# A planned order for attention and SwiGLU: PSUM banks given out one by one, and offsets for five stages

## The chip, the cores and the metric

The kernel runs on one core of a Trainium2 chip. Time is device time in microseconds (us), from the start of an execution to its end. The engines are TensorE (PE: matmuls and transposes; its weight loads, PEld, have rows of their own), VectorE (DVE), ScalarE (ACT), GpSimd (POOL) and SyncE (SP, which here only issues DMAs). Each engine works through its own list of instructions in order and waits on semaphores. TensorE writes to PSUM, which has eight banks of 512 fp32 columns by 128 partitions here; VectorE and ScalarE empty them.

## What is computed

Eight batches of eight heads, 576 positions, head size 64, in fp32:

```python
scores = scale * np.matmul(q, k.transpose(0, 1, 3, 2))
thresh = np.max(scores, axis=-1, keepdims=True) - tau
scores = np.where(scores >= thresh, scores, -1000000000.0)
attn = np.exp(scores - max); attn = attn / (sum(attn) + 1e-09)
x = (attn @ v), heads joined: 4608 rows of 512
xn = x / sqrt(mean(x * x) + 1e-06) * rms_g
g = xn @ w_gate; val = xn @ w_val            # 512 -> 1536
out = (g * sigmoid(g) * val) @ w_out         # 1536 -> 512
```

(The last lines of the softmax and the joining of heads are shortened here.)

## The kernel before

**Work units.** The 4608 rows are cut into 36 chunks of 128 rows: for each batch four chunks of main rows, and for each pair of batches one chunk ("v") made of the last 64 rows of both. A chunk has four steps, one per pair of heads, so there are 144 steps. A step is:

- Scores (L697, `emit_burst`): fp32 matmuls of 64x64 tiles into `s_ps[0]` and `s_ps[1]`, one tile per head, 576 columns each. For steps 0 to 31 a burst is one step; from step 32 on scores are cut into bursts of 1024 columns without regard to steps (`CHOP`, `plan_bursts` L743). A burst fills two banks of each head, and its matmuls follow one another on PE.
- Row maxima (L730, `ttr`): VectorE reads the scores from PSUM, writes them negated and scaled to `ssb`, and takes the extreme in the same instruction (`mx`, or `mxp` where a step's row is cut by a burst).
- Threshold (L771, `nthr`, POOL), masking (L782, `prelu`, ACT), exponential to fp16 (L789, `ex2`, ACT).
- Transposes of the weights `wsb` to `wt`: for the first 16 steps on TensorE (L834, copied out by VectorE, L843), then by DMA (L849).
- For each two steps: attention times v (L870 and L875, `emit_av`), with the row sums in an extra column, and division by them on VectorE (L892, L893).

After a chunk's four steps `emit_x` (L900) squares and sums (ACT, L910), takes the power (POOL), scales (POOL) and transposes x to `xnT` by DMA. The chunks form ten groups (`SIZES`: 2, 2 and eight times 4). `emit_ffn` takes a group at a time: 12 slices of the hidden size, each with a gate product (L976, `gmm`) and a value product (L981, `vmm`), tanh on ACT (L990), two VectorE instructions (L993 `silu`, L998 `gate`) to `hf`, and then per chunk 12 output products in two runs of six (L1047, `omm`), a copy (L1062 or L1064, `ev`) and a store. In the last group output products are streamed slice by slice (L1022). Weights come in by 12 loads of 512 KB and are cast on POOL (L1133); `wo` comes by POOL's own DMAs (L1145).

The start has a path of its own (`emit_first`, L422): loads of batch 0, transposes on TensorE (L462), copies by ACT and DVE (L472). `setup` (L287) zeroes a tile for eight warm-up matmuls (L291, L292, L299) and fills constant columns of `va` (L309 to L311, `vconst`).

**PSUM.** Score banks are two tiles of 1024 columns, so four banks. The other four are the "ring", which serves transposes, attention outputs and FFN products. After the last step's maxima the score banks are opened to the ring as well (`OPENS`); `SLOTS` and `ACC` say which banks ordinary users and the streamed last group may have. Semaphores between engines follow the data in the banks; the planner below decides order and bank numbers only.

**The planner.** Nothing is emitted directly. Each piece of work is an `Op` with an engine, an estimated cost, a due time `prio` (in steps), and dependences. `order_ops` (L56) simulates the engines: at each point, the operation that can start first goes next, and where several of an engine can start at the same moment, the one with the lowest `prio`. To `prio` the table `RANK` adds an offset per engine and kind of work, one number for all of the run, for due times of 8 and later; SP's operations get none. FFN slices have due times of their own: group by group, never before the step after which the group is complete plus `LAG` 8, 12 slices over 16 steps for a full group. A change between fp32 score matmuls and other kinds is charged `SWITCH`. Bursts depend on all maxima of the burst before (`last_ttr`), a maximum on the whole burst (`made`). A user of the ring gets the bank that has been free longest. In the end the operations' functions are called in the planned order, which fixes every engine's list.

Of the kernel before, what the change touches and what calls it, by code (L numbers as in the profile page):

```python
# [23 lines left out]
SWITCH = 125.0  # L24

RANK = dict(
    ACT={"emit_ffn/ev": 450, "emit_ffn/store": 110, "emit_ffn/tanh": -300, "emit_k_tail/ev": -210, "emit_q_tail/ev": -80, "emit_qk/ev": 370,
        "emit_softmax/ex2": 60, "emit_softmax/prelu": 220, "emit_x/sq": -330},
    DVE={"emit_blocks/turn_k": 120, "emit_blocks/turn_kt": 288, "emit_blocks/turn_q": 293, "emit_burst/ttr": -57.4, "emit_ffn/ev": 320,
        "emit_ffn/gate": 60, "emit_ffn/silu": -59, "emit_k_tail/ev": 80, "emit_qk/ev": -20, "emit_softmax/ev": 320, "emit_x/ev": 50},  # L30
    PE={"emit_av/fn": -370, "emit_burst/fn": 16, "emit_ffn/gmm": 20, "emit_ffn/omm": 23, "emit_ffn/vmm": -40, "emit_k_tail/tr": 210, "emit_q_tail/tr":
        -160, "emit_qk/tr": 60, "emit_softmax/tr": -40, "emit_x/trp": 20},
    POOL={"emit_block_loads/swap": 40, "emit_softmax/nthr": -240, "emit_x/mean": -150, "emit_x/norm": -10, "round_/<lambda>": 130, "main/<lambda>":
        700, "main/cast": -280},
# [3 lines left out]
class Op:  # L38
    __slots__ = ("eng", "cost", "prio", "deps", "fn", "ring", "frees", "slot", "end", "start", "dma", "opens", "nring", "mode", "bulk", "release", "pick", "quad", "lat")

    def __init__(self, eng, cost, prio, deps, fn, ring=None, frees=None, dma=0.0, nring=1, mode=0, bulk=False):
        self.eng, self.cost, self.prio, self.fn = eng, cost, prio, fn
        self.deps = [d for d in deps if d is not None]
        self.ring, self.frees, self.dma = ring, frees, dma
        self.slot = self.end = self.start = None
        self.opens = ()
        self.nring = nring
# [8 lines left out]
def order_ops(ops, ring_sizes):  # L56
# [4 lines left out]
    for o in ops:  # L61
        if o.prio >= 8.0 and o.eng != "SP":
            path = o.fn.__qualname__.split(".")
            o.prio += RANK.get(o.eng, {}).get((path[-3] if path[-3].startswith(("emit", "load", "setup", "transposed", "round")) else "main") + "/" + path[-1], 0.0)

    ring_free = {r: [(0.0, i) for i in range(n)] for r, n in ring_sizes.items()}
    users = {}
    left = {}
    for i, o in enumerate(ops):
        left[i] = len(o.deps)  # L70
        for d in o.deps:
            users.setdefault(id(d), []).append(i)
# [10 lines left out]
    while len(out) < len(ops):  # L83
# [35 lines left out]
        if o.ring is not None:  # L119
# [5 lines left out]
            if o.pick:  # L125
                o.slot.sort()
# [1160 lines left out]
```

## Time and profile before

Three runs took 533.15, 534.36 and 535.47 us; the median is 534.36. The profiled execution's own span, from its first instruction to its last, is 532.2 us; the median lies 2.2 us above it, which takes in what lies around the instructions and the difference between executions.

| | before |
|---|---|
| span of the profiled execution | 532.2 us |
| median of three runs | 534.36 us |
| PE busy | 521.9 us (98%) |
| DVE busy | 465.9 us (88%) |
| ACT busy | 443.6 us (83%) |
| POOL busy | 224.9 us (42%) |
| mean granted TensorE clock | 0.997 |
| instructions | 14401 |
| longest chain, share by engine | PE 68%, DVE 11%, ACT 10%, no visible wait 4%, DMA 3% |

A profile row gives a line of the kernel, engine, operation, what it writes and reads, a count, busy time and the mean of one; then idle time before it on its engine and what ended that. Matmuls are pipelined and the end of one is modelled, so rows of consecutive matmuls overlap and PE looks busier than it is. The time from one start to the next is more reliable, and the chain of waits gives it: there each piece is cut where the next begins. "PEld <- DVE" is a weight load that waited for VectorE. "issue" is time for which the profile shows no wait.

### The profile page before, as it was taken

The page shows a single profiled execution, that of the slowest core. Times are in us where ns is not written, and L with a number is a line of the kernel's source. Part 1 is how long each engine was busy: PE and PEld are TensorE (multiplying, and loading weights), DVE is VectorE, ACT ScalarE, POOL GpSimd, SP SyncE. Part 2 cuts the span into 40 slices and gives each one's busy share as a digit, 9 for nine tenths or more (in the row PEclk, how much of TensorE's full clock was granted, in tenths as well). Part 3 has the DMA queues.
Part 4 walks back from the last instruction along what each step waited for, and adds up shares of the span by engine and source line. Part 5 has one row for each costly group of instructions (what it writes and reads, how often), then busy time and mean ns, then how long its engine had stood idle before and what let it go on. Part 6 is the DMA issues. An engine that isn't in the chain of part 4 may idle for free.

```text
span 532.2 us, 14401 instructions
## 1 busy us (share of the span) xinstructions
PE 521.9 (98%) x5368; PEld 275.4 (52%) x5368; DVE 465.9 (88%) x1348; ACT 443.6 (83%) x648; POOL 224.9 (42%) x478
## 2 busy tenths in 40 slices
PE   8999999999999999999999999999999999999996
PEld 4666666654555454545454544454545454454442
DVE  4899989979999799989997999999999898865741
ACT  5999999989997899889987898989999999962210
POOL 2368777424762165727733265726662111111000
PEclk9999999999999999999999999999999999999998
DMA  9999999979977788999889898999897678653013
GB/s 196 237 282 289 239 159 180 182 150 230 181 162 165 166 170 182 157 223 182 170 167 180 146 175 174 203 210 166 174 195 137 119 118 134 128 112 70 13 29 99
DMA packets 218886, 88.51 MB, mean 166 GB/s; under 512 B 195264, under 2 KB 204992, under 8 KB 218816
## 3 DMA queue, kind: packets, MB, share of 16 engines
q1 hardware_dynamic: 216016, 85.49, 81.1%
q0 software_dynamic: 1600, 1.57, 1.9%
q8 instruction: 42, 0.69, 0.5%
q10 hardware_dynamic: 1200, 0.52, 0.5%
q14 instruction: 28, 0.23, 0.1%
HBM read 37.75 MB, written 9.44 MB: 89 GB/s over the span
## 4 chain that ended last, share of the span: by engine, by line
PE 68%; DVE 11%; ACT 10%; issue 4%; DMA 3%; POOL 1%; SPq 1%; DVEq 0%; ACTq 0%; POOLq 0%
PE s_ps L697 21%; PE ring L1047 13%; PE ring L981 11%; PE ring L976 11%; DVE ssb L730 6%; ACT ssb L782 5%; PE ring L875 4%; ACT wsb L789 3%; PE s_ps L1022 2%; ACT th L990 2%; DVE sl L993 2%; PE ring L870 1%; DMA stg<-in_moe_w_gate_dram 1%; DMA wt<-wsb 1%; PE s_ps L981 1%
## 5 line engine op out<-in xcount | busy, mean ns | idle before, releaser
L782 ACT ACTIVATE ssb<-ssb,nth 128x576 f32<-128x576 f32 x288 | 209.3, 766 | 21.5 <-POOL nth L771 21.0
L730 DVE CUSTOM_DVE_ANT_0 ssb<-s_ps,zcol 128x576 f32<-128x576 f32 (+8 forms) x288 | 169.5, 636 | 6.3 <-PE s_ps L697 5.5
L697 PE MATMUL s_ps<-qkt 64*64 64x288 f32 (+8 forms) x2256 | 170.8, 412 | 1.1 <-DVE mx L730 0.8
L789 ACT ACTIVATE wsb<-ssb 128x1152 f16<-128x1152 f32 x144 | 166.7, 1158 | 2.5 <-DMA wt<-wsb 0.3
L697 PEld LDWEIGHTS s_ps<-qkt 64*64 64x64 f32 x2256 | 81.9, 134 | 66.4 <-issue 28.2
L976 PE MATMUL ring<-xnT,wg 128*128 128x512 f16 (+1 forms) x464 | 109.2, 358 | 0.6 <-DVE sl L993 0.5
L981 PE MATMUL ring<-xnT,wv 128*128 128x512 f16 (+1 forms) x456 | 106.9, 357 | 0.5 <-DVE sl L993 0.2
L990 ACT ACTIVATE th<-ring 128x512 f32<-128x512 f32 (+1 forms) x116 | 62.5, 541 | 39.4 <-PE ring L976 39.0
L771 POOL TENSOR_SCALAR nth<-mx 128x2 f32<-128x2 f32 x144 | 31.0, 215 | 151.0 <-DVE mx L730 141.0
L993 DVE SCALAR_TENSOR_TENSOR sl<-th,ring 128x512 f32<-128x512 f32 (+1 forms) x116 | 72.1, 623 | 11.3 <-ACT th L990 11.2
L981 PEld LDWEIGHTS <-wv 128*128 128x128 f16 x480 | 44.6, 98 | 50.2 <-issue 11.1
L976 PEld LDWEIGHTS <-wg 128*128 128x128 f16 x480 | 43.0, 98 | 52.6 <-issue 15.1
L730 DVE CUSTOM_DVE_ANT_0 ssb<-s_ps,zcol,mxp 128x128 f32<-128x128 f32 (+7 forms) x112 | 52.9, 510 | 13.2 <-PE s_ps L697 13.0
L875 PE MATMUL ring<-va,wt 128*128 128x65 f16 (+1 forms) x1280 | 51.1, 193 | 0.0
L875 PEld LDWEIGHTS <-wt 128*128 128x128 f16 (+1 forms) x1280 | 46.1, 100 | 5.0 <-issue 0.6
L1047 PE MATMUL ring<-wo,hf 128*128 128x512 f16 x204 | 47.7, 379 | 0.0
L998 DVE TENSOR_TENSOR stg<-ring,sl 128x512 f16<-128x512 f32 (+1 forms) x57 | 35.6, 628 | 2.4
L998 DVE TENSOR_TENSOR hf<-ring,sl 128x512 f16<-128x512 f32 (+1 forms) x57 | 35.5, 627 | 1.8
L1047 PE MATMUL ring<-wo,stg 128*128 128x512 f16 x156 | 36.5, 379 | 0.0
L390 POOL COPY spare<-qkx 32x576 f32<-32x576 f32 x48 | 31.7, 660 | 6.5 <-DMA qkx<-in_k_dram 2.5
L893 DVE TENSOR_TENSOR xsb<-ring,rz 128x256 f32<-128x256 f32 x72 | 30.6, 425 | 3.5
L1047 PEld LDWEIGHTS <-hf 128*128 128x128 f16 x216 | 20.0, 98 | 25.9 <-issue 3.5
(75 smaller groups left out, 485.1 us busy)
## 6 DMA issues: line engine op xcount, KB each, us to landing
vst<-in_v_dram SPq DMA_DIRECT2D x32, 256.0 KB, 4.1
qkx<-in_k_dram SPq DMA_DIRECT2D x24, 288.0 KB, 3.4
qkx<-in_q_dram SPq DMA_DIRECT2D x24, 288.0 KB, 3.6
out_dram<-osb SPq DMA_DIRECT2D x48, 128.0 KB, 2.6
stg<-in_moe_w_gate_dram SPq DMA_DIRECT2D x6, 512.0 KB, 6.5
stg<-in_moe_w_val_dram SPq DMA_DIRECT2D x6, 512.0 KB, 6.3
wt<-wsb SPq DMA_TRANSPOSE x128, 3.6
out_dram<-osb SPq DMA_DIRECT2D x8, 256.0 KB, 3.0
```

The source lines that it names most:

```text
L390: nc.gpsimd.tensor_copy(out=dst, in_=at)
L697: nc.tensor.matmul(s_ps[h][rows, at:at + hi - lo], lhs(hs), k_of(bb, p, h)[hs, lo:hi], start=True, stop=True)
L730: nc.vector.tensor_tensor_reduce(out=ssb_of(s)[:, h, lo:hi], in0=s_ps[h][:, at:at + hi - lo], in1=zcol.to_broadcast([128, hi - lo]), scale ...
L782: nc.scalar.activation(out=sb_[:, h], in_=sb_[:, h], func=PRELU, scale=-1.0, bias=nth[m][:, h:h + 1], **PRELU_KW)
L789: nc.scalar.activation(out=wsb[s % NW], in_=sb_, func=AF.Exp)
L875: nc.tensor.matmul(ring[o.slot[0]][rs, at:at + D + 1], w[:, 5 * h + j, rs], va[vi][:, p, 2 * j + h], start=False, stop=(h == 1 and j == 3))
L976: nc.tensor.matmul(ring[o.slot[0]][:, 0:n], wg[d][:, fs], xnT[slot][:, d, 0:n], start=(d == 0), stop=(d == 3))
L981: nc.tensor.matmul(ring[o.slot[0]][:, 0:n], wv[d][:, fs], xnT[slot][:, d, 0:n], start=(d == 0), stop=(d == 3))
L990: nc.scalar.activation(out=th[i][:, 0:n], in_=ring[g.slot[0]][:, 0:n], func=AF.Tanh, scale=0.5)
L993: nc.vector.scalar_tensor_tensor(out=sl[i][:, 0:n], in0=th[i][:, 0:n], scalar=1.0, in1=ring[g.slot[0]][:, 0:n], op0=ALU.add, op1=ALU.mult)
L998: nc.vector.tensor_tensor(out=hf[hi][:, 0:n], in0=ring[vv.slot[0]][:, 0:n], in1=sl[i][:, 0:n], op=ALU.mult)
L1047: nc.tensor.matmul(ring[(first or o).slot[0]], hf[hs[fc][0]][:, 128 * j:128 * (j + 1)], wo[:, fc], start=(fc == 0), stop=(fc == NFC - 1))
```

## The change

Banks: the two score tiles become three banks wide, and two separate banks remain, so that all eight are one row with numbers: 0, 1, 2 and 3, 4, 5 in the tiles, 6 and 7 alone. Scores still use 1024 columns: banks 0, 1, 3, 4. The planner keeps a free time for each bank. A burst claims each bank that it writes, and may be placed when each will be free at the moment that it is first written (`lead`), not when all of the burst before is done. A maximum depends on the burst's runs up to its own columns, and the last maximum on a bank opens it. Users of the ring take, among banks that are free, the one with the lowest `ORDER`; before a score bank's first claim they may have it too. `LEND` and `long` have an effect only for bursts wider than 1024 columns.

Ranks: `RANK` has five numbers for each kind, for due times below 8, to 24, to 40, to 140 and beyond. They apply to all operations with a due time above -400, so also to the set-up; bursts' later runs and some early transposes are below that and keep theirs.

Further: `GATE = 0.0` makes a gate product depend on the scores of the step that its due time names, where that is one of the 144; `SWITCH` is 145; knobs that were zero are dropped; `NSB = 3` names the number of `ssb` buffers, which was 3. Kinds and numbers of instructions stay.

The diff, cut:

```diff
-SWITCH = 125.0
-
+SWITCH = 145.0
+
+PHASES = (8.0, 24.0, 40.0, 140.0)
+NO_RANK = (0.0,) * 5
 RANK = dict(
-    ACT={"emit_ffn/ev": 450, "emit_ffn/store": 110, "emit_ffn/tanh": -300, "emit_k_tail/ev": -210, "emit_q_tail/ev": -80, "emit_qk/ev": 370,
-        "emit_softmax/ex2": 60, "emit_softmax/prelu": 220, "emit_x/sq": -330},
-    DVE={"emit_blocks/turn_k": 120, "emit_blocks/turn_kt": 288, "emit_blocks/turn_q": 293, "emit_burst/ttr": -57.4, "emit_ffn/ev": 320,
-        "emit_ffn/gate": 60, "emit_ffn/silu": -59, "emit_k_tail/ev": 80, "emit_qk/ev": -20, "emit_softmax/ev": 320, "emit_x/ev": 50},
-    PE={"emit_av/fn": -370, "emit_burst/fn": 16, "emit_ffn/gmm": 20, "emit_ffn/omm": 23, "emit_ffn/vmm": -40, "emit_k_tail/tr": 210, "emit_q_tail/tr":
-        -160, "emit_qk/tr": 60, "emit_softmax/tr": -40, "emit_x/trp": 20},
-    POOL={"emit_block_loads/swap": 40, "emit_softmax/nthr": -240, "emit_x/mean": -150, "emit_x/norm": -10, "round_/<lambda>": 130, "main/<lambda>":
-        700, "main/cast": -280},
+    ACT={
+        "emit_ffn/ev": (0, 0, 0, 83.3, 0),
+        "emit_ffn/store": (0, 0, 0, 0, 216.8),
+        "emit_ffn/tanh": (-348.2, 2.2, -292.1, 225.3, 0),
+        "emit_k_tail/ev": (4.4, 0, 0, 0, 0),
+        "emit_q_tail/ev": (0, 148.7, 0, 0, 0),
+        "emit_qk/ev": (-294.7, -680.2, 0, 0, 0),
+        "emit_softmax/ex2": (688.9, -374.1, 204, 144.3, -50.5),
+        "emit_softmax/prelu": (-142.9, 742, -203.1, 409.5, 631.3),
+        "emit_x/sq": (-93.3, -306.1, 89.6, -383.1, 134.1),
+        "load_k/load": (355.8, 0, 0, 0, 0),
+        "transposed/ev": (407.3, 0, 0, 0, 0),
+    },
+    DVE={
+        "emit_av/half": (-104.9, -428.2, 139.8, 73.8, -228.9),
+        "emit_blocks/turn_k": (0, 354.1, 1986.6, 2718.1, 0),
+        "emit_blocks/turn_kt": (0, 88.2, 176.4, 686.3, 0),
+        "emit_blocks/turn_q": (0, 371.2, 405.2, 771.2, 0),
+        "emit_burst/ttr": (-185.6, -651.8, -3224, 629.7, 15.2),
+        "emit_ffn/ev": (300.5, -91.9, -300.9, -267.6, 0),
+        "emit_ffn/ev_half": (0, 0, 0, 347.2, 0),
+        "emit_ffn/gate": (0, -35.1, -183.1, 21.9, -127.8),
+        "emit_ffn/silu": (0, -880.8, -253.5, 179.5, 4.2),
+        "emit_k_tail/ev": (42, 0, 0, 0, 0),
+        "emit_qk/ev": (254.3, 136.3, 0, 0, 0),
+        "emit_softmax/ev": (261, -259.2, 0, 0, 0),
+        "emit_x/ev": (334.1, -66.6, 0, 0, 0),
+        "setup/consts": (-279.2, 0, 0, 0, 0),
+        "setup/vconst": (84.8, 0, 0, 0, 0),
+        "setup/zero": (451.9, 0, 0, 0, 0),
+        "transposed/ev": (414.3, 0, 0, 0, 0),
+    },
+    PE={
+        "emit_av/fn": (-434.3, 261.7, -112.9, -161.6, -129.4),
+        "emit_burst/fn": (143.3, 133.1, 5.4, -132.4, 66.2),
+        "emit_ffn/gmm": (0, 207.5, -221.9, -423.7, 298),
+        "emit_ffn/omm": (0, 1652.9, 2477.1, 159.6, 300),
+        "emit_ffn/vmm": (0, 332.2, 360.7, -118.5, -265.4),
+        "emit_softmax/tr": (142.9, 229.8, 0, 0, 0),
+        "emit_x/trp": (-271.9, -255.5, 0, 0, 0),
+        "setup/warm": (-330.7, 0, 0, 0, 0),
+        "transposed/tr": (99.5, 0, 0, 0, 0),
+    },
+    POOL={
+        "emit_block_loads/swap": (0, -351.4, 244.2, 1627.1, 0),
+        "emit_softmax/nthr": (273.6, -394.6, -503.4, 366.1, 0),
+        "emit_x/mean": (577, 135.3, 81.4, -265.2, 182),
+        "emit_x/norm": (-417.5, 266.4, 326.7, 244.3, 192.7),
+        "main/<lambda>": (0, 159.9, 0, 0, 0),
+        "main/cast": (363.9, 214, 0, 0, 0),
+        "round_/<lambda>": (52.7, 93.4, -30.8, 307.2, 0),
+        "setup/<lambda>": (-738.6, 0, 0, 0, 0),
+    },
...
-def order_ops(ops, ring_sizes):
+def order_ops(ops):
 
 
     import heapq
 
     for o in ops:
-        if o.prio >= 8.0 and o.eng != "SP":
+        if o.eng != "SP" and o.prio > -400.0:
             path = o.fn.__qualname__.split(".")
-            o.prio += RANK.get(o.eng, {}).get((path[-3] if path[-3].startswith(("emit", "load", "setup", "transposed", "round")) else "main") + "/" + path[-1], 0.0)
-
-    ring_free = {r: [(0.0, i) for i in range(n)] for r, n in ring_sizes.items()}
+            name = (path[-3] if path[-3].startswith(("emit", "load", "setup", "transposed", "round")) else "main") + "/" + path[-1]
+            o.prio += RANK.get(o.eng, {}).get(name, NO_RANK)[sum(o.prio >= c for c in PHASES)]
+
+    free_at = {b: 0.0 for b in range(BANKS)}
+    claims_left = {b: 0 for b in range(BANKS)}
+    for o in ops:
+        for b, _ in o.claims:
+            claims_left[b] += 1
+    lent = {b: 0 for b in range(BANKS)}
+
+    def lendable(o):
+        if o.pick:
+            return [b for b in free_at if b in o.pick]
+        return [b for b in free_at if not claims_left[b] and (b in SLOTS or len(out) < n_open[0]) or claims_left[b] and (
+            lent[b] < LEND and not o.long or not_yet[b])]
+
+    not_yet = {b: True for b in range(BANKS)}
+    n_open = [len(ops)]
     users = {}
     left = {}
+    for o in ops:
+        o.deps = [d for x in o.deps for d in (x if isinstance(x, list) else [x]) if d is not None]
...
-                    free = [f for f in ring_free[o.ring] if f[1] in (o.pick or SLOTS)]
+                    free = sorted(free_at[b] for b in lendable(o))
                     if len(free) < o.nring:
                         continue
-                    t = max(t, sorted(free)[o.nring - 1][0])
+                    t = max(t, free[o.nring - 1])
+                if o.claims:
+                    if any(b not in free_at for b, _ in o.claims):
+                        continue
+                    t = max([t] + [free_at[b] - lead for b, lead in o.claims])
...
-                got = min(f for f in ring_free[o.ring] if f[1] in (o.pick or SLOTS))
-                ring_free[o.ring].remove(got)
-                o.slot.append(got[1])
+                got = min(lendable(o), key=lambda b: (max(free_at[b] - t, 0.0), ORDER[b], b))
+                del free_at[got]
+                lent[got] += 1
+                o.slot.append(got)
             if o.pick:
                 o.slot.sort()
+        for b, _ in o.claims:
+            del free_at[b]
+            claims_left[b] -= 1
+            not_yet[b] = False
...
-            ring_free["R"].append((o.end + LAT[o.eng], o.frees[0].slot[o.frees[1]]))
-        for slot in o.opens:
-            ring_free["R"].append((o.end + LAT[o.eng], slot))
+            free_at[o.frees[0].slot[o.frees[1]]] = o.end + LAT[o.eng]
+        for b in o.opens:
+            free_at[b] = o.end + LAT[o.eng]
+            lent[b] = 0 if o.long else LEND
+            if not any(claims_left.values()):
+                n_open[0] = 0
...
-    s_ps = [ps(f"s_ps{h}", 1024) for h in range(2)]
+    osb += [ssb[i % NSB][:, i // NSB, 0:DM] for i in range(4)]
+
+    s_ps = [ps(f"s_ps{h}", 1536) for h in range(2)]
     ROW_AT = 512 - S // 2
-    ring = [ps(f"ring{i}", 512) for i in range(4)]
-    ring += [s_ps[h][:, 512 * i:512 * (i + 1)] for h in range(2) for i in range(2)]
+    ring = [s_ps[h][:, 512 * i:512 * (i + 1)] for h in range(2) for i in range(3)]
+    ring += [ps(f"ring{i}", 512) for i in range(BANKS - 6)]
...
+        seg_run = [max(i for i, run in enumerate(runs) for y, a, b, _ in run if y == s and lo <= a < hi) for s, lo, hi, _ in segs]
         no_whole = any(w is None for _, w, _ in info.values())
-        deps = [x for d, _, _ in info.values() for x in d] + last_ttr
+        deps = [x for d, _, _ in info.values() for x in d] + last_burst
...
-            if not made and REL_N[0] <= prio < REL_N[1]:
-                o.release = REL[0] + REL[1] * prio
+            if not made:
+                lead, first = 0.0, {}
+                for r in runs:
+                    for _, lo, hi, at in r:
+                        for bank in range(at // 512, (at + hi - lo - 1) // 512 + 1):
+                            first.setdefault(bank, lead)
+                    lead += 9.0 + (COST["s_virt"] if no_whole else COST["s_main"]) * sum(hi - lo for _, lo, hi, _ in r) / S
+                o.claims = [(3 * h + bank, first[bank]) for bank in first for h in range(2)]
...
-                t = ttr_of[s, h] = add("DVE", 75.0 + (hi - lo) / 0.96, s - 1 + (TTR_PRIO if s >= TTR_FROM else TTR_EARLY) - (TTR_E if s < TTR_TO else 0.0), made + [o_c] + held + before, ttr)
-                last_ttr.append(t)
-
-    last_ttr = []
+                t = ttr_of[s, h] = add("DVE", 75.0 + (hi - lo) / 0.96, s - 1 + TTR_EARLY, made[:seg_run[n_] + 1] + [o_c, held] + before, ttr)
+                t.long = sum(hi - lo for _, lo, hi, _ in segs) > 1024
+                t.opens = [3 * h + bank for bank, last_ in done_by.items() if last_ == n_]
...
+            if pr - GATE < len(steps):
+                gates.append((g, pr - GATE))
...
-        ttr_of[len(steps) - 1, h].opens = OPENS[h]
-    seq = order_ops(ops, {"R": 4})
+    seq = order_ops(ops)
...
 PACE = 16.0
+GATE = 0.0
 HOLD = {}
-TTR_E = 0.0
-TTR_TO = 16
 SQ_DVE = (0,)
 OUT_DVE = (1,)
 LAGS = ()
-CHOP = ((32, 144),)
-TTR_PRIO = 0.0
+CHOP = ((32, 144, 1024),)
 TTR_EARLY = 1.0
-TTR_FROM = 0
 BY_ROW = 4
-SLOTS = (0, 1, 2, 3, 4, 6)
-ACC = (4, 5, 6, 7)
-OPENS = ((4, 5), (6, 7))
+BANKS = 8
+LEND = 1
+ORDER = (0, 1, 3, 0, 1, 3, 2, 2)
+SLOTS = (0, 2, 3, 5, 6, 7)
+ACC = (0, 1, 3, 4)
+NSB = 3
...
-REL = (0.0, 0.0)
-REL_N = (0, 0)
```

## The prediction

> **What bounds the kernel now.** I read the page's busy shares and its 40 slices first, then the busy time by stretches of the run, the chain that ended last, and the waits of TensorE's weight loads.
>
> ```profile
> PE 521.9 (98%) x5368; PEld 275.4 (52%) x5368; DVE 465.9 (88%) x1348; ACT 443.6 (83%) x648; POOL 224.9 (42%) x478
> PEclk9999999999999999999999999999999999999998
> ```
>
> TensorE has a record open for 98% of the span at full clock, and no other engine comes near that. But ends of matmuls are modelled, so the share must be checked against durations. The chain gives them; each piece there is cut where the next one begins (start, length, line, count).
>
> ```profile
> 45.33 1.20 PE s_ps L697 x16
> 264.41 1.89 PE s_ps L697 x32
> 266.30 0.97 PE ring L976 x4
> 267.27 0.86 PE ring L981 x4
> 268.13 2.59 PE ring L1047 x12
> ```
>
> A score burst of 1024 columns takes 1.89 us; the bursts of one step (576 columns, x16 in the chain) come as short as 1.13. So a column costs (1.89 - 1.13)/448 = 1.70 ns and a burst 0.15 beside that, and the four products after it cost 0.97 instead of 0.86: 0.26 per burst for changing kinds. TensorE's own work follows: 144 steps x 0.977 = 140.7; 95 bursts (32 single ones, 112 x 576/1024 = 63 wide) x 0.26 = 24.7; gate and value products, 8 groups x 24 x 0.86 = 165.1 and two groups of half the width, 20.6; output products, 72 x 1.29 (half of the 2.59 above) = 92.9; attention times v, 72 pairs x 0.60, and about 1 more for steps of two batches = 44; transposes about 16; warm-up 3.6. Sum 508. The span is 532.2: 24 us are not TensorE work. 1.2 lie before its first instruction and 5.0 after its last one (527.2), so some 18 are idle time that the modelled ends hide.
>
> Where they lie comes from the stretches (us, length; then busy PE, PEld, DVE, ACT, POOL with counts, clock, DMA share, GB/s).
>
> ```profile
> 0.00:20.00 20.00, 18.42 (x154) 10.11 (x155) 11.51 (x37) 13.38 (x25) 4.88 (x16) 1.00 1.00 197
> 20.00:40.00 20.00, 18.68 (x257) 13.84 (x257) 18.76 (x54) 18.85 (x27) 11.99 (x25) 1.00 1.06 280
> 40.00:60.00 20.00, 19.63 (x269) 13.57 (x265) 18.87 (x55) 18.96 (x30) 16.81 (x30) 1.00 1.09 296
> 60.00:80.00 20.00, 19.82 (x254) 13.59 (x247) 18.56 (x55) 19.65 (x33) 13.58 (x27) 1.00 0.96 163
> 80.00:100.00 20.00, 20.00 (x251) 12.88 (x249) 19.90 (x58) 19.83 (x33) 12.04 (x25) 1.00 1.04 176
> 100.00:460.00 360.00, 358.19 (x3822) 180.18 (x3820) 337.37 (x1022) 328.99 (x467) 162.10 (x349) 1.00 0.89 170
> 460.00:520.00 60.00, 60.00 (x355) 28.17 (x354) 38.38 (x70) 22.92 (x37) 3.53 (x9) 1.00 0.31 64
> ```
>
> Counting the instructions of each kind in these stretches with the durations above, TensorE works 88 to 89 us of the first 100, about 355 of the 360 up to 460, and without a gap from there to its end. Two regimes, then. Up to 100 us softmax sets the pace: from 20 to 100, ACT is idle for 2.7 us in all and DVE for 3.9, and one step of attention takes about 3.05 us. From 100 on TensorE sets it, with products of two groups still to do when the last scores are done (463 us), so what TensorE loses anywhere before is not won back later.
>
> **The ceiling.** The same instructions run, on the same engines, in the same number of score bursts: wide bursts stay 1024 columns, and bank numbers cost nothing. So only idle time can be won. Ahead of 20 us: the first softmax starts at 10.07 after load, transposes, scores and maximum; I allow 1. From 20 to 100: no more than ACT's idle 2.7, say 3. From 100 to 460: 6 at most. After that nothing; the 5.0 behind the last product are two copies and a store, untouched. Together 10.
>
> **Part by part.** *Bank-wise claims and the maximum's shorter dependence.* The planner had started a burst when every maximum of the burst before was done, and a maximum when the whole burst was; now it goes by bank. Semaphores on the chip follow data in both versions; the order of PE and DVE is what moves. It shows its worth where steps are latency-bound: burst 1.20, two maxima 0.76 + 0.67, with two hand-overs of 0.1 to 0.4, is about 3 us, which is the 3.05 per step. But DVE fills that loop with other work and ACT is full, so it can win only the 3 us of that stretch. From 100 on TensorE has products to do while a burst waits.
>
> ```profile
> PEld s_ps L697 <- DVE mxp L730: 7.0, 17, 0.5
> PEld L870 <- DMA wt<-wsb: 0.8, 1, 0.8
> PE ring L976 <- DVE sl L993: 0.5, 1, 0.5
> ```
>
> In the waits from 100 to 460 (total, times, longest), a burst's weights waited for a maximum 17 times, 0.41 each, and a product group for a bank of the ring once. The first of these rows is what bank-wise claims aim at, and it can also grow (third rival).
>
> *Choice of bank.* The one free longest gave way to a fixed preference (6, 7, then 2, 5 while scores last). A bank that was just emptied may be taken at once. Bounds: 0, and 0.5 (the row above) for each of 232 product groups, 116 us if all waited; I take the row's single wait, so 0. Before the first burst, transposes now take the score banks first, and that burst waits till they are copied out: 0 to 0.7 (a copy there took 0.62 to 0.69); covered by the warm-up's delay below, so 0.
> The Trainium skill's page "Perfetto Trace Analysis", section "Matmuls", speaks against this edit: independent matmul groups should rotate through the banks, so that evacuation of one overlaps the next. By that rule some groups would wait; with one in ten at 0.5 I would add 12 us. This trace has the wait once among 232, with the rotation in place, so it can't show what its absence costs.
>
> *Ranks of the first stage.* Ranks now reach steps below 8 and the set-up. On DVE the filling of va (rank to -5) then stands ahead of the zeroing that the warm-up needs (rank to +252), and both are ready at the start. The va memsets took 1.25 to 3.05, 1.80 us, so the warm-up, which began at 1.22, begins near 3.0 and its 3.4 us (eight at 0.43) end at 6.4; the first transposes, at 4.46 now, queue behind it on PE, and behind them the first scores (6.93), maxima, ACT's first softmax and the loads of q and k that reuse those buffers on SP's queue. Cost 0 to 1.85. Part is covered: the second step's scores wait for a load and copies until 9.64, and copies that ACT does between 10 and 17 (0.65 + 0.35 + 0.46) can move into the hole. I take 1.2.
>
> *GATE = 0.* A gate product now waits for the scores of the step in its own due time. It binds where TensorE ran ahead of that: at 160 us 36 gate products were issued, the last due at 53.7, against about 50.4 steps of scores. 3.3 steps x 0.75 x 1.72 (one gate and value pair) = 4.3 us of TensorE work pushed back there. What covers it is output work, which the new ranks hold back in steps 8 to 40 (+1653, +2477) and which had all been issued by 120 us. Bounds 0 and 4.3; I take 0, because held-back work of that size exists (4 chunks, 10.4 us).
>
> *Ranks of the other stages.* They only decide between operations ready together. From step 40 on the maximum stands last but for the transposes by DVE (+630 against -268 to +180 for what empties the ring), and TensorE prefers gate products (-424). What ACT and POOL reorder (prelu +410, the threshold +366) leads to the same softmax and lies beside TensorE's backlog; without that backlog, one late softmax would cost up to 2.2 (the longest wait of the masking step for its threshold). SP has no ranks: its weight loads, stores and DMA transposes move with what releases them; price 0 to 0.8, the one wait for wt in the rows above; I take 0. SWITCH 145, the dropped knobs and buffers renamed by NSB change no instruction.
>
> The sum: a better order wins between 0 and 10; no row puts it nearer to one end, so the middle, 5; the front costs 1.2: -3.8 us. The profiled span of 532.2 becomes 528.4; around it lie 2.2 to the median of 534.36, which gives 530.6.
>
> **The rivals.** *No change that can be told:* gains between 100 and 460 stay small, because 355 of 360 us are work, and the front eats what the softmax stage wins. 532 to 537. A measurement of this kernel tells about 0.5%, 2.7 us, from no change.
> *The planner reaches the ceiling:* all 10 won, front covered: 524. For it: offsets per stage can serve both regimes; against it: ACT full from 20 to 100.
> *The burst waits inside itself (slower):* a burst is now started when its first bank is free and the second is expected to be by the time it is written. Its matmuls stand back to back on PE, so if a maximum comes late, all products queued behind wait. Since maxima now rank low on DVE, which is 94% busy from 100 to 460, they come late more often. At 0.41 for each of the 63 - 17 wide bursts that don't wait today: +19 us, less the 3.8: 549. It decides from 10 more waiting bursts on (3.8/0.41). Against it: today 17 of 63 wait, with maxima in front.
> *The gate has no cover:* 4.3 lost against the 3.8: about 535 at full price once, near 539 if it recurs from 200 to 270 us, where scores and due times also run level.
>
> **How the numbers follow.** Forecast (a gain of 2.7 to 7): 0.34; the ceiling case 0.12; no change 0.20; gate without cover, beyond 537, 0.12; waits inside bursts or for rings 0.22. Faster 0.46, same 0.20, slower 0.34. The range goes from 523 to 547: the ceiling with 1 us to spare, and the third rival up to 40 of its 46 bursts; about 0.1 lies above and 0.05 below. The forecast's own range is 527 to 531.7.
>
> **What the changed profile would show.** The warm-up starts near 3.0 and ACT's first softmax at 11 to 12, not 10.07; if it is still 10, the front's step is wrong. From 20 to 100, ACT's idle time falls under 2 us and scores of step 32 come before 100. From 100 to 460, the waits of burst weights for mxp stay under 7 us if I am right; 15 or more says third rival. Output products appear between 120 and 165 us if the gate is covered. The last score burst, at 463 now, ends near 460, and the tail stays gapless. I am wrong if TensorE's idle time between 100 and 460 grows beyond 10 us.

## The result

The changed kernel takes 684.88 us (median of four runs, 680.97 to 688.8), against 534.32 before (median of four): 1.281 times as long, 95% interval 1.274 to 1.289. The profiled execution spans 679.3 us. 530.6 was predicted, in a range of 523 to 547. The loss of 150.6 us is about eight times the 19 us at which the slower rival priced bursts that wait inside themselves, and it has several causes that had each been priced at little or nothing.

### The profile page after: what moved, and what is told of

Read it like the earlier page. It is cut to its first block, busy times and chain, and to the rows that moved or that the text cites. A ratio compares the mean times of both kernels' runs of the same rounds, so it can differ in the third digit from the quotient of the medians.

```text
span 679.3 us, 14488 instructions
## 1 busy us (share of the span) xinstructions
PE 568.3 (84%) x5384; PEld 281.4 (41%) x5384; DVE 478.8 (70%) x1348; ACT 453.8 (67%) x648; POOL 223.9 (33%) x478
## 4 chain that ended last, share of the span: by engine, by line
PE 63%; DVE 27%; issue 5%; ACT 3%; POOL 0%; DVEq 0%; POOLq 0%
PE s_ps L776 27%; DVE ssb L819 16%; PE ring L1141 7%; PE s_ps L1073 5%; PE s_ps L1068 5%; PE ring L1068 4%; PE ring L1073 4%; PE s_ps L1141 3%; DVE sl L1087 2%; PE s_ps L967 2%; DVE xsb L985 2%; PE s_ps L1116 2%; ACT th L1084 2%; DVE stg L1092 1%; DVE hf L1092 1%
## 5 line engine op out<-in xcount | busy, mean ns | idle before, releaser
L776 PE MATMUL s_ps<-qkt 64*64 64x288 f32 (+9 forms) x2272 | 202.0, 421 | 65.7 <-DVE mx L819 23.5
L819 DVE CUSTOM_DVE_ANT_0 ssb<-s_ps,zcol 128x576 f32<-128x576 f32 (+8 forms) x288 | 172.9, 636 | 36.3 <-PE s_ps L776 16.6
L776 PEld LDWEIGHTS s_ps<-qkt 64*64 64x64 f32 (+1 forms) x2272 | 83.9, 134 | 154.7 <-DVE mx L819 44.0
L819 DVE CUSTOM_DVE_ANT_0 ssb<-s_ps,zcol,mxp 128x128 f32<-128x128 f32 (+7 forms) x112 | 54.6, 515 | 48.5 <-PE s_ps L776 42.5
L1068 PE MATMUL ring<-xnT,wg 128*128 128x512 f16 (+1 forms) x300 | 72.6, 365 | 0.4 <-DVE sl L1087 0.4
L1073 PEld LDWEIGHTS <-wv 128*128 128x128 f16 x480 | 43.5, 97 | 64.2 <-issue 27.7
L1073 PE MATMUL ring<-xnT,wv 128*128 128x512 f16 (+1 forms) x276 | 66.0, 362 | 0.9 <-DVE stg L1092 0.9
L1073 PE MATMUL s_ps<-xnT,wv 128*128 128x512 f16 (+1 forms) x204 | 47.2, 353 | 10.1 <-DVE mx L819 8.3
L1087 DVE SCALAR_TENSOR_TENSOR sl<-th,ring 128x512 f32<-128x512 f32 (+1 forms) x75 | 47.8, 639 | 5.8 <-ACT th L1084 5.7
L1068 PE MATMUL s_ps<-xnT,wg 128*128 128x512 f16 (+1 forms) x180 | 40.6, 348 | 8.7 <-DVE mx L819 3.7
L1087 DVE SCALAR_TENSOR_TENSOR sl<-th,s_ps 128x512 f32<-128x512 f32 (+1 forms) x45 | 27.3, 608 | 24.8 <-ACT th L1084 12.8
L468 POOL COPY qkx<-spare 32x576 f32<-32x576 f32 x48 | 31.7, 661 | 3.0
L468 POOL COPY qkx<-qkx 32x576 f32<-32x576 f32 x48 | 31.6, 659 | 3.0
```

What stands on the lines that cost most here:

```text
L468: nc.gpsimd.tensor_copy(out=dst, in_=at)
L776: nc.tensor.matmul(s_ps[h][rows, at:at + hi - lo], lhs(hs), k_of(bb, p, h)[hs, lo:hi], start=True, stop=True)
L819: nc.vector.tensor_tensor_reduce(out=ssb_of(s)[:, h, lo:hi], in0=s_ps[h][:, at:at + hi - lo], in1=zcol.to_broadcast([128, hi - lo]), scale ...
L1068: nc.tensor.matmul(ring[o.slot[0]][:, 0:n], wg[d][:, fs], xnT[slot][:, d, 0:n], start=(d == 0), stop=(d == 3))
L1073: nc.tensor.matmul(ring[o.slot[0]][:, 0:n], wv[d][:, fs], xnT[slot][:, d, 0:n], start=(d == 0), stop=(d == 3))
L1087: nc.vector.scalar_tensor_tensor(out=sl[i][:, 0:n], in0=th[i][:, 0:n], scalar=1.0, in1=ring[g.slot[0]][:, 0:n], op0=ALU.add, op1=ALU.mult)
```

## The profile after

The busy line of the page:

```profile
PE 568.3 (84%) x5384; PEld 281.4 (41%) x5384; DVE 478.8 (70%) x1348; ACT 453.8 (67%) x648; POOL 223.9 (33%) x478
```

The stretches (us, length; busy PE, PEld, DVE, ACT, POOL with counts, clock, DMA share, GB/s):

```profile
0.00:20.00 20.00, 15.03 (x99) 7.74 (x100) 7.53 (x26) 9.58 (x20) 4.40 (x14) 1.00 0.94 200
20.00:100.00 80.00, 61.03 (x749) 39.77 (x749) 54.82 (x154) 57.40 (x82) 40.20 (x77) 0.96 0.72 173
100.00:460.00 360.00, 298.87 (x3008) 144.18 (x3008) 273.14 (x804) 264.52 (x374) 139.16 (x294) 1.00 0.71 140
```

TensorE's count of instructions is 5384 where it was 5368, so "kinds and numbers of instructions stay" holds for the other engines only; how some score products are cut depends on the order. No engine is the bound any more: TensorE, at 98% before, has 84%, in a span that is 147 us longer. PE is busy for 15.0 us in the first 20 where it was for 18.4, and for 61 from 20 to 100 where it was for 78; between 100 and 460 PE has a record open for 299 of 360 us where it had 358, DVE falls from 337 to 273 and ACT from 329 to 265. When all engines idle more at once, they wait for one another. The waits say for what (engine, line, tile, what it waited for; total us, times, longest).

```profile
ACT ssb L874 <- POOL nth L863: 83.7, 56, 3.8
DVE ssb L819 <- PE s_ps L776: 59.1, 70, 3.9
PEld s_ps L776 <- DVE mx L819: 44.0, 48, 2.2
...
PE s_ps L776 <- DVE mx L819: 23.5, 36, 1.4
PEld s_ps L776 <- DVE xsb L985: 23.1, 24, 1.6
...
DVE rz L984 <- PE s_ps L776: 20.4, 23, 2.2
...
PEld s_ps L776 <- DVE sl L1087: 14.6, 11, 2.1
...
PE s_ps L1073 <- DVE mx L819: 8.3, 16, 0.8
```

L776 is the score burst (L697 before), L819 the maximum, L984 and L985 the division of attention, L1073 the value product, L1087 the first FFN instruction on VectorE. Four of these rows name pairs that have nothing to do with each other: a burst has no use for x or for sl, a division none for scores, a value product none for a maximum. What they share is the tile `s_ps`. In the kernel before the same waits of a burst are small (a wait for several events is put down to the one that came last), and its divisions wait for their own products:

```profile
PEld s_ps L697 <- DVE mx L730: 6.0, 18, 0.6
PEld s_ps L697 <- DVE xsb L893: 3.8, 9, 0.4
DVE rz L892 <- PE ring L875: 0.8, 2, 0.6
PEld s_ps L697 <- DVE sl L993: 0.8, 3, 0.4
```

The chain of the changed kernel shows such a stretch (start, length; each piece cut where the next begins).

```profile
200.69 1.96 PE s_ps L776 x24
202.64 0.17 DVE rz L984
...
202.84 0.42 DVE xsb L985
203.26 0.66 DVE ssb L819
...
204.61 0.54 DVE ssb L819
...
205.21 1.04 PE s_ps L1068 x4
...
209.12 0.61 DVE sl L1087
...
209.77 0.77 PE s_ps L776 x8
```

The division at 202.64 reads attention from the third bank of a score tile; those products were done when the burst began at 200.69, and yet it comes after the burst, which writes the first two banks (VectorE stood still 0.28 us before it, and 1.31 before the next division, at 208.41). The gate product at 205.21 goes to a third bank, and stands until the last maximum on the other banks is done. The burst at 209.77 waits 1.43 us for the FFN instruction that empties a third bank. Each such wait stops a queue, and the next one starts from there.

## The experiments

Five things could be at work: the tile (theory A), the new order as a whole (B), the ranks (R), the maximum's rank in particular (M), and the planning bank by bank, which lets a burst stop in its middle (P).

**The tile.** The third banks become tiles of their own; each engine's order stays as in the changed kernel. In this run and the next two, every engine's list in the built program is, instruction for instruction, that of the kernel it is compared with, so the tiles are all that differs.

```diff
-    s_ps = [ps(f"s_ps{h}", 1536) for h in range(2)]
+    s_ps = [ps(f"s_ps{h}", 1024) for h in range(2)]
...
-    ring = [s_ps[h][:, 512 * i:512 * (i + 1)] for h in range(2) for i in range(3)]
-    ring += [ps(f"ring{i}", 512) for i in range(BANKS - 6)]
+    apart = [ps(f"ring{i}", 512) for i in range(4)]
+    ring = [x for h in range(2) for x in (s_ps[h][:, 0:512], s_ps[h][:, 512:1024], apart[h])] + apart[2:]
```

> The changed kernel with the two third score banks (2 and 5) made separate PSUM tiles of their own; every engine's list of work and every bank number stay as in the changed kernel. Theory A (work on a ring bank that lies in the same tile as the score banks waits for scores and maxima that it has nothing to do with): the 150 us go, 525 to 545. Theory B (the new order itself, its ranks and gate, starves the engines): 650 to 690, as the changed kernel.

582.5 us, 1.090 times before (1.087 to 1.094). 102.3 us go with the tile (the changed kernel's own runs spread over 8), and 48 stay: A and B are both right in part, and neither's number was met. The four unrelated pairs are gone from the waits, while the wait of a burst's weights for a maximum stays, at 43.6 us after 44.0:

```profile
PEld s_ps L776 <- DVE mx L819: 43.6, 58, 1.6
```

That the banks lie elsewhere in PSUM doesn't explain it: a maximum over 576 columns takes 636 ns in the kernel before, 636 in the changed one and 635 here. What goes is waiting, not slower work.

The converse puts two of the ring's four banks into the score tiles of the kernel before.

```diff
-    s_ps = [ps(f"s_ps{h}", 1024) for h in range(2)]
+    s_ps = [ps(f"s_ps{h}", 1536) for h in range(2)]
...
-    ring = [ps(f"ring{i}", 512) for i in range(4)]
+    ring = [s_ps[h][:, 1024:1536] for h in range(2)] + [ps(f"ring{i}", 512) for i in range(2)]
```

> The kernel before, order and ranks untouched; two of its four ring banks are put into the score tiles as their third banks. Theory A: most of the loss appears with no other change, 610 to 700. Theory B: 533 to 537, as before.

703.5 us (1.317), just above A's range: 169 us from the tiles alone, with the order before. Its waits have the same unrelated pairs. The kernel before shows the first with 0.8 us in 3 waits, and the other two not at all:

```profile
PEld s_ps L697 <- DVE sl L993: 21.8, 24, 1.7
...
DVE sl L993 <- PE s_ps L697: 18.1, 16, 2.5
...
PE s_ps L981 <- DVE mx L730: 16.3, 22, 1.7
```

A half dose, with bank 2 in its score tile and bank 5 apart, in the changed kernel:

```diff
+    s_ps = [ps(f"s_ps{h}", (1536, 1024)[h]) for h in range(2)]
+    apart = [ps(f"ring{i}", 512) for i in range(3)]
+    thirds = (s_ps[0][:, 1024:1536], apart[2])
```

> The changed kernel with only one of the two third banks (bank 2) in a score tile and bank 5 apart. Theory A: a dose between, 570 to 650. Theory B: 650 to 690.

646.1 us (1.209): one bank makes 63.5 of the 102.3. The compiled programs tell why. I counted the waits whose awaited instruction touches the same PSUM tile, but no bank in common and no other memory in common:

```
kernel before            195   (96 bursts or maxima each way)
changed kernel           478
changed, banks apart     239
changed, one bank shared 380
before, banks shared     548
```

So in these programs a wait is set by the tile, not by the bank. (These are counts from the programs, not from a trace; another rule of counting moves each number, but not their order.) The kernel before has such waits too, between a burst and the maxima of the burst before, but its planner puts those in that order anyway.

**The ranks alone**, in the kernel before, with SWITCH 145; the look-up is the changed one.

```diff
-SWITCH = 125.0
+SWITCH = 145.0
+PHASES = (8.0, 24.0, 40.0, 140.0)
...
+            o.prio += RANK.get(o.eng, {}).get(name, NO_RANK)[sum(o.prio >= c for c in PHASES)]
```

> The kernel before with its old banks and its planner, but the five-stage ranks and SWITCH 145; no gate, no bank-wise claims. Theory A: no shared tile, so 525 to 550. Theory B (ranks are the cause): 600 or more.

588.1 us (1.101; 1.098 to 1.104): the ranks lose 54 without any of the banks, with SWITCH in it, which alone costs 7 (below). Theory A had 525 to 550, B 600 or more; neither was met.

**Two by two**, with the third banks apart: planning by bank or by whole bursts, new ranks or old. Planning by bank with the old ranks, for every kind of work, and no gate (the line of the maximum stands for all):

```diff
-        "emit_burst/ttr": (-185.6, -651.8, -3224, 629.7, 15.2),
+        "emit_burst/ttr": (0, -57.4, -57.4, -57.4, -57.4),
...
-GATE = 0.0
+GATE = -1000.0
```

> Third banks in tiles of their own; planner with claims bank by bank, old ranks (one number per kind, due times from 8 on), no gate. Theory R (the new ranks make what is left of the loss, 48 us): 530 to 545. Theory P (planning bank by bank orders a burst's later part behind a maximum of the same tile, so that the burst waits inside itself): 560 to 590.

599.2 us (1.121): theory P's range was 560 to 590, R's 530 to 545. The new ranks are not what is left of the loss; with this planner they win. The gate off, with the new ranks:

```diff
-GATE = 0.0
+GATE = -1000.0
```

> Third banks apart, claims bank by bank, new ranks, no gate. If the gate is behind the remaining loss, 535 to 550; if it costs the 4.3 us of the prediction, 576 to 580; theories R and P both say 570 to 590.

588.2 us (1.100). So in the bank-wise planner the new ranks win 11.0 (599.2 to 588.2) and the gate 5.6 (588.2 to 582.5), against the sign that I had for each. Planning by whole bursts with the new ranks and the gate:

```diff
-                            first.setdefault(bank, lead)
+                            first.setdefault(bank, 0.0)
...
-                t = ttr_of[s, h] = add("DVE", 75.0 + (hi - lo) / 0.96, s - 1 + TTR_EARLY, made[:seg_run[n_] + 1] + [o_c, held] + before, ttr)
+                t = ttr_of[s, h] = add("DVE", 75.0 + (hi - lo) / 0.96, s - 1 + TTR_EARLY, made + [o_c, held] + before, ttr)
```

> Third banks apart, new ranks and gate, but the planner counts as the chip's waits do: a burst after all maxima of the burst before, a maximum after the whole burst. Theory R: 575 to 595, near the ranks alone (588). Theory P: 530 to 550.

586.1 us (1.097), as R said for this planner; P's 530 to 550 did not come. The fourth corner has the same two lines, the old ranks and no gate:

> Third banks apart, whole bursts, old ranks, no gate. What stays of the change is the choice of bank by ORDER, early lending and SWITCH 145. If the fixed choice costs nothing: 532 to 538; if each product group pays for a bank just emptied: 545 or more.

548.8 us (1.027). From there the new ranks and gate lose 37; planning by bank loses 50; both together lose 34. They were not two losses to add: each is a loss alone, and the ranks and the gate mend part of what the planning breaks.

**Which edit of the planning.** From the 599.2 of planning by bank with the old ranks, each of the two lines of the diff above is undone alone. First the claims lose their lead, and the maximum keeps its short dependence on the parts of the burst that it reads:

```diff
-                            first.setdefault(bank, lead)
+                            first.setdefault(bank, 0.0)
```

> Third banks apart, old ranks, no gate (claims by bank with both edits: 599; with neither: 549). Here only the maximum's edit: it depends on the burst's runs up to its own columns; a burst is placed after all maxima of the burst before. Theory P (a later run of the burst is emitted behind a maximum that reads the same tile, so the burst stops in its middle): 580 to 600, with waits of burst weights for a finished maximum near 60 us. If the other edit is the cause: 545 to 555.

600.0 us (1.124). Then the claims keep their lead, and the maximum depends on the whole burst:

```diff
-                t = ttr_of[s, h] = add("DVE", 75.0 + (hi - lo) / 0.96, s - 1 + TTR_EARLY, made[:seg_run[n_] + 1] + [o_c, held] + before, ttr)
+                t = ttr_of[s, h] = add("DVE", 75.0 + (hi - lo) / 0.96, s - 1 + TTR_EARLY, made + [o_c, held] + before, ttr)
```

> The same with only the other edit: a burst may be placed when its first bank is free and the second will be when it is first written; a maximum depends on the whole burst. Theory P: 547 to 560, since the burst's first matmul waits for the last maximum of the tile and is planned up to 0.9 us too early. If this edit is the cause: 580 to 600.

546.6 us (1.024). All of the 50 us comes with the maximum's short dependence; the lead's 2.2 (546.6 against 548.8) lie within the two intervals. The waits of the former, then of the latter:

```profile
PEld s_ps L768 <- DVE mx L811: 59.3, 79, 1.6
...
PE s_ps L768 <- DVE mx L811: 27.3, 49, 0.8
```
```profile
PEld s_ps L768 <- DVE mx L811: 9.8, 21, 1.2
...
PE s_ps L768 <- DVE mx L811: 2.5, 5, 0.7
```

How it looks in time is seen in the changed kernel with banks apart (rows of PE and DVE; in brackets the idle time before, and what ended it):

```profile
260.08 1.97 PE L776 MATMUL s_ps<-qkt 64*64 64x320 f32 x24
...
262.20 0.55 DVE L819 CUSTOM_DVE_ANT_0 ssb<-s_ps,zcol,mxp 128x320 f32<-128x320 f32 x1
...
262.68 0.08 DVE L819 DVE_READ_ACCUMULATOR2_ANT mx<- 128x1 f32 x1
262.81 0.21 PEld L776 LDWEIGHTS s_ps<-qkt 64*64 64x64 f32 x8 [1.43 <-DVE mx L819]
262.81 0.45 PE L776 MATMUL s_ps<-qkt 64*64 64x128 f32 x8 [0.76 <-DVE mx L819]
```

A burst of 1024 columns is cut into 320, 576 and 128. The planner lets the maximum of the first 320 go while the burst still runs, so that maximum is emitted before the burst's last part. Both touch the same tile, one the first bank and the other the second, and the last part waits for the maximum. The burst that took 1.89 us before is spread over 3.2, PE stands with all that is queued behind it, and the second head's maximum, which begins at 263.33, is late in its turn. Not run: the same order with each score bank a tile of its own, which would tell whether the short dependence pays once its waits go by bank.

**Which rank.** New ranks below 40 and old ones from 40 on, for every kind of work, in the kernel before. Against the run with all ranks new (the line of the maximum stands for all):

```diff
-        "emit_burst/ttr": (-185.6, -651.8, -3224, 629.7, 15.2),
+        "emit_burst/ttr": (-185.6, -651.8, -3224, -57.4, -57.4),
...
```

> The kernel before with its own banks and planner, SWITCH 145 and the new ranks for due times below 40 only; from 40 on the old ones. All five stages together gave 588. If the first stages carry that loss: 565 to 588; if steps 40 to 140 do, as theory M says (maxima ranked last on VectorE there, so score banks are emptied late and the burst waits): 535 to 550, of which some 3 to 5 from the first softmax being 2.9 us later.

545.9 us (1.022). And all ranks new, except the maximum's from 40 on, against the same run:

```diff
-        "emit_burst/ttr": (-185.6, -651.8, -3224, 629.7, 15.2),
+        "emit_burst/ttr": (-185.6, -651.8, -3224, -57.4, -57.4),
```

> The kernel before with all new ranks except one: the maximum's rank for due times from 40 on is the old -57. Theory M: 540 to 560, and the burst weights' waits for a partial maximum (35.9 us in 29 with all new ranks) fall below 12. If no single rank is behind it: 575 to 590.

546.4 us (1.023). One operation's rank in the last two stages, two numbers out of some two hundred, carries 42 of the 54 us; theory M holds, though the waits for mxp fell to 12.4 us, just over the 12 that were expected. The waits with all ranks new, then with that one set back:

```profile
PEld s_ps L745 <- DVE mxp L778: 35.9, 29, 3.6
...
PE s_ps L745 <- DVE mxp L778: 25.5, 14, 3.3
```
```profile
PEld s_ps L745 <- DVE mxp L778: 12.4, 25, 1.8
...
PE s_ps L745 <- DVE mxp L778: 2.1, 3, 1.3
```

The same number set back in the changed kernel with banks apart:

> The changed kernel with the third banks apart (582.5) and the maximum's rank from 40 on set back to -57. If that rank costs here what it costs in the planner before (42 us): 540 to 550. If, beside bursts that stop in their middle, a late maximum matters little or an early one stops them more often: 575 to 600.

599.9 us (1.124), 17 worse. A late maximum that falls behind the burst's end would stop it less, and the waits fit that: with the early one, matmuls and weights of bursts waited for a finished maximum 85.3 us, with the late one 63.5. Both rows' sums overlap in time; only their order is read from them.

**What the 549 still had.** Two edits of that kernel: the bank that has been free longest, and no lending before the first burst.

```diff
-                got = min(lendable(o), key=lambda b: (max(free_at[b] - t, 0.0), ORDER[b], b))
+                got = min(lendable(o), key=lambda b: (free_at[b], b))
```

> Third banks apart, whole bursts, old ranks, no gate (548.8 as it was), and a user of the ring takes the bank that has been free longest instead of the fixed preference. If the preference cost the 14 us: 534 to 538; if it cost nothing: 546 to 551.

```diff
-            lent[b] < LEND and not o.long or not_yet[b])]
+            lent[b] < 0)]
```

> The same kernel of 548.8 with its fixed preference, but score banks are not lent before their first burst. Its first softmax came at 15.3 us, 5.2 later than before. If lending is behind that: first softmax near 10, and 541 to 545; if the lateness has another cause, or is made up later: 547 to 551.

545.9 (1.022) and 541.0 us (1.013). Without lending the first softmax comes at 9.76 us instead of 15.32, and 7.7 us are won. The free-longest choice is 2.8 faster, which lies within the two intervals, and its first softmax also comes earlier, at 12.20; so the fixed preference costs the later run nothing that these runs show.

**Small edits of the kernel before.** The gate alone; the bank-wise code with its lead, the rest set as before; and the switching price alone:

```diff
+            if pr < len(steps):
+                gates.append((g, pr))
```

> The kernel before with the gate alone: a gate product depends on the scores of the step of its due time. The prediction's bounds for the gate were 0 to +4.3 us, 0 taken: 534 to 539. In the changed kernel with banks apart it won 5.6 us (588.2 without, 582.5 with), so with this order it may win: 526 to 533.

540.7 us, 1.013 (1.011 to 1.015).

Against the changed kernel, whose third banks are apart and ranks old besides:

```diff
-SWITCH = 145.0
+SWITCH = 125.0
...
-            lent[b] < LEND and not o.long or not_yet[b])]
+            lent[b] < 0)]
...
-                got = min(lendable(o), key=lambda b: (max(free_at[b] - t, 0.0), ORDER[b], b))
+                got = min(lendable(o), key=lambda b: (free_at[b], b))
...
-                t = ttr_of[s, h] = add("DVE", 75.0 + (hi - lo) / 0.96, s - 1 + TTR_EARLY, made[:seg_run[n_] + 1] + [o_c, held] + before, ttr)
+                t = ttr_of[s, h] = add("DVE", 75.0 + (hi - lo) / 0.96, s - 1 + TTR_EARLY, made + [o_c, held] + before, ttr)
...
-GATE = 0.0
+GATE = -1000.0
...
-TTR_EARLY = 1.0
+TTR_EARLY = 0.0
```

> The kernel before with one edit of the change that was not seen to cost anything: a burst may be placed when its first bank is free and the second will be when it is first written. All else as before: whole-burst maxima, old ranks, the bank free longest, no lending, no gate, SWITCH 125, the maximum due when it was. In the other setting the edit won 2.2 us (546.6 against 548.8). If that carries over: 529 to 533; if the kernel before is a local best that any new order leaves: 536 to 542.

541.1 us, 1.014 (1.011 to 1.017). This is not the lead alone, as the expectation has it: with the lead taken out, the bank-wise code still plans another order than the code before.

```diff
-SWITCH = 125.0
+SWITCH = 145.0
```

> The kernel before with SWITCH 145 in the place of 125, a number that the planner alone uses. The prediction priced it at nothing: 532 to 536. If the order before stands on such numbers, so that any of them changed loses some of it: 537 to 543.

541.0 us, 1.014 (1.012 to 1.016). Three edits of different kinds, each within 0.5 us of the same +7. Each is under 2%, but clear of the kernel before. The switching price is a number that no instruction carries. Its trace, of the longest of its four runs (542.8), shows where it went. The stretches from 20 to 463, the start of the last scores before:

```profile
20.00:100.00 80.00, 76.42 (x992) 52.66 (x990) 73.32 (x210) 73.97 (x115) 52.78 (x101) 0.98 0.98 224
100.00:463.00 363.00, 357.60 (x3803) 180.75 (x3805) 336.58 (x1021) 329.04 (x467) 161.14 (x348) 1.00 0.89 169
```

The one long stop of a burst, among the rows of PE in time:

```profile
125.40 3.01 PE L697 MATMUL s_ps<-qkt 64*64 64x384 f32 x32 [2.73 <-DVE mxp L730]
```

Before, PE was busy for 78.12 and 361.19 in these stretches. So 1.7 and 3.6 are lost, 2.7 of the latter in one stop at 125 us, and the last scores begin at 468.6 instead of 463.3: 5.3 later, the sum of the two. The span is 8.8 longer (541.0 against 532.2), so another 3.5 come after the last scores. So the order before is better on the chip than these three neighbours. Why it is better by 7 us was not shown.

## Why the prediction was wrong

The loss in one row of runs, from the kernel before: 534 to 549 with whole bursts, old ranks, SWITCH 145, the maximum's due time one step later, fixed preference and lending; 599 with planning by bank; 588 with the new ranks; 583 with the gate; 685 with the shared tiles. The first of these steps is not taken apart to the end: without lending it is 541, and SWITCH alone takes the kernel before from 534 to 541.

- *"Bank numbers cost nothing".* The step that failed most: 102 us. That the instructions stay doesn't say that their waits do. "Semaphores on the chip follow data in both versions" (and "follow the data in the banks", in the part on the kernel before) was wrong: in these programs they follow the tile. The trace before could have raised the question, since it never had scores and ring in one tile while both were in use, so "nothing" had no row behind it. The split kernel, its converse and the half dose show it.
- *Bank-wise claims, "can win only the 3 us".* They lost 50, all by the maximum's short dependence. The ceiling was reasoned for gains; I gave this edit no bound on the other side but in the third rival. That rival named the place, a burst that waits inside itself, and missed both the reason (it blamed maxima ranked low; they help there) and the number (46 waits of 0.41, so 19).
- *"They only decide between operations ready together."* True of the planner, and no bound: which of two ready operations goes first on DVE, all through the run, was worth 42 us through the maximum's rank alone. "Without that backlog, one late softmax would cost up to 2.2" priced one occurrence.
- *The first stage, 0 to 1.85, 1.2 taken.* The warm-up began at 3.08 as said (3.0). But the first softmax came at 13.05 with the early ranks in the planner before, 3.0 us later where 1.85 was the bound, and at 15.13 in the changed kernel, not at 11 to 12. Lending, with the old ranks, puts it at 15.32 (9.76 without): transposes are lent the score banks and stand before the first burst. Lending had been priced at 0 "covered by the warm-up's delay"; it cost 7.7 without that delay.
- *Gate, 0 to 4.3, 0 taken.* +6.7 in the kernel before and -5.6 in the changed one with banks apart: an interval for one order says nothing of another.
- *"SWITCH 145, the dropped knobs ... change no instruction."* SWITCH alone: +7.0, and TensorE's count fell from 5368 to 5360. Of the dropped knobs, `TTR_PRIO` and `TTR_FROM` were zero and yet at work: with them the maximum was due at step s - 1, and without them `TTR_EARLY`, 1.0, makes it s. No run takes this alone.
- *Choice of bank, 0 taken.* 2.8 at most, within the intervals, and all of it may be the front. The Trainium skill's page "Perfetto Trace Analysis", section "Matmuls", would have groups rotate through the banks; the 12 us that I had estimated by it are not there. The row was nearer.
- *The ceiling of 10.* No run contradicts it: none beats the kernel before. What it didn't give is a floor. That TensorE worked 355 of 360 us meant that a new order had 5 us to win there and had no bound on its loss, and I put the chance of slower at 0.34.

Of the forecast signs, the one on mxp didn't decide: from 100 to 460 bursts' weights waited 9.3 us for it, between the marks of 7 and 15, and it was mx that grew, from 0.4 to 28.4. The others did: TensorE's visible idle time between 100 and 460 went from 2 to 61 us where 10 was the limit, ACT's idle time from 20 to 100 from 2.7 to 22.6 where under 2 was forecast, and the last score burst began at 606.6. Output products did appear between 120 and 165 us, from 141 on, as the gate's cover asked.

## What to carry to other kernels

Before two users share a PSUM tile, look at the waits of the compiled program: banks that are separate in the chip's work may be one thing to the framework that sets the semaphores, and a planner that knows better than they do orders work into stalls. In a kernel where the bound engine works 98% of its time, a change of order can't win more than the idle time left, but it can lose far more (54 us here by ranks alone); each re-ordering needs a bound on that side too. Take a planner's edits one by one: here two of them (ranks and gate) mended part of what a third (the maximum's short dependence) broke, and only their differences showed it.

## Unexpected on the chip

TensorE's granted clock did not go by its idle time in all. In the changed kernel it was 0.96 from 20 to 100 us, where PE was busy for 61 of 80 us; before, it was 1.00 there, with 78. But in the half dose it was 1.00 with 64, and 0.999 over a run of which PE was busy for 85%. Where it fell, it fell for a short time: with SWITCH 145 it was 0.50 from 126.7 to 130.1 us, just after the one stop of 2.73 us, and 1.00 before and behind:

```profile
122.00:126.00 4.00, 1.27 (x13) 0.72 (x13) 2.88 (x13) 3.79 (x7) 1.86 (x5) 1.00 0.90 225
126.70:130.10 3.40, 3.40 (x39) 2.23 (x32) 1.57 (x5) 2.66 (x4) 0.21 (x1) 0.50 1.19 239
130.10:134.00 3.90, 3.90 (x26) 1.30 (x25) 2.98 (x12) 3.90 (x6) 2.63 (x5) 1.00 1.11 278
```

With the ranks alone, whose bursts' longest wait for a maximum was 3.6 us, the mean was 0.971 to 0.976 in all four runs, against 0.997 before. That single stops and not their sum set it off is not shown: with the ranks alone a stop of 2.62 us that ended at 249.7 had 1.00 behind it. In the changed kernel's profiled run it is a small part of the loss, with a mean of 0.993 for all of it.
